# Batch 0's k loaded as fp32 by the SP queue and converted by VectorE, in a fused attention and feed-forward kernel on one core

## The chip, the cores and the metric

The kernel runs on one core of one Trainium2 chip. The metric is the device time of one execution in microseconds; lower is better. Before the change, three runs gave 164.0, 164.4 and 165.47 us, so the median is 164.4. One further execution was recorded by the hardware profiler; all rows shown here come from it.

## The reference

An attention over 32 learned memory slots, then a feed-forward layer with a maximum over three projections:

```python
batch, n_heads, seq, head_dim, n_mem = 8, 8, 576, 64, 32
a = softmax(phi, axis=slots)                       # fp32 [8, 8, 576, 32]
k_m = einsum('bhsm,bhsd->bhmd', a, k)
v_m = einsum('bhsm,bhsd->bhmd', a, v)
attn = softmax(q @ k_m.T / sqrt(head_dim), axis=slots)
x = (attn @ v_m)                                   # as [4608, 512]
h = max(x @ w1, x @ w2, x @ w3)                    # w1, w2, w3: [512, 768]
out = h @ w_out                                    # w_out: [768, 512]
```

All inputs and the output are fp32 in HBM. The matrix products run in bf16.

## The kernel before

**Tiling.** A batch has eight heads, taken as four pairs j. `by_pair` (L79) lays a batch of q, k, v or phi out as 128 partitions by four pairs; in each pair a partition holds nine rows in a row, for q, k and v 576 numbers, which is 2304 bytes of fp32. k and v go to `kvo`, a bf16 tile for each of two alternating batches; row 1 of it is k, row 0 is v, and row 2 is a column of ones. q goes to `qq`, phi to `ph` (fp32).

**Weights.** `w_sb` (L71) holds w1, w2 and w3 as bf16, as four pairs by three matrices by 768 columns, so that in each partition the three matrices alternate from pair to pair. `wo_sb` holds w_out. At the start of the run w3 is transposed on TensorE (step W, L186, matmuls at L192), and w3 times w_out is formed (step O, L197, matmuls at L200), which then serves all batches. w1 and w2 are needed by the folds (step D, matmuls at L445).

**Queues.** A load that converts fp32 to bf16 goes through the software DMA queue, which GpSimd (POOL) feeds; each such load is an instruction in GpSimd's own order. The SP queue carries phi of batch 0 (two halves, L92) and later every output row (L552). Both queues run on the same 16 DMA engines.

**Order.** The whole program is one hand-written list of steps (L621 on), each a letter, a number and a batch. The list fixes every engine's own order; an instruction then waits only for what it needs. The steps of the opening that matter here:

- E: the exponential of phi on ScalarE (L234).
- H0, H2 (`load_kv`, L96): the two halves of batch 0's k, pairs 0 and 1, then pairs 2 and 3. H1 and H3 are the halves of v. L3 (`load_q`, L108) loads q.
- Z: so many matmuls on a zero tile (`warm_up`, L163), which nothing reads.
- B0, N0, K0 (L243, L267, L297): the product of exp(phi) with k and the column of ones on TensorE (L254), its normalisation on VectorE, its transpose. B1, N1 and K1 do the same with v.
- Q0, Q1 (L311): transposes of q on VectorE (L318). S, M, R, X: scores, their exponential, sums and normalisation.
- Y2, Y3, Y0, Y1 (`load_w`, L115, and `load_wo`, L123): the loads of w3, w_out, w1, w2.
- G0 (`wait_for`, L128): a copy of two numbers of k on GpSimd, so that the loads issued behind it start only when batch 0's k has landed.
- L0 to L3: loads for the next batches.

GpSimd's order in the opening is therefore: k (two halves), q, the identity matrix and some constants, w3, the gate, w_out, v (two halves), w1, w2, then phi, k, q and v of batch 1.

Of the kernel before, what the change touches and what calls it, by code (L numbers as in the profile page):

```python
# [8 lines left out]
FP32 = mybir.dt.float32  # L9
# [6 lines left out]
def kernel(  # L16
# [12 lines left out]
    nc = tc.nc  # L29

    B, H, S, D = q.shape
# [5 lines left out]
    NC = S // HP  # L37
# [26 lines left out]
    kvos = []  # L64
# [6 lines left out]
    w_sb = const.tile([P, NP, 3, DF], BF16, name="w_sb")  # L71
# [5 lines left out]
    loaded = {}  # L77

    def by_pair(src, b):  # L79
        return src[b].rearrange("h s d -> (h s) d").rearrange(  # L80
            "(j p c) d -> p j (c d)", p=P, c=NC
        )

    halves = [slice(0, NP // 2), slice(NP // 2, NP)]

    def load_ph(b):
        ph = inp.tile([P, NP, NC, M], FP32, name="ph")
        loaded.setdefault(b, {})["ph"] = ph
        dst = ph.rearrange("p j c m -> p j (c m)")
        if b == 0:  # L90
            for h in halves:
                nc.sync.dma_start(out=dst[:, h], in_=by_pair(phi, b)[:, h])  # L92
        else:
            nc.gpsimd.dma_start(out=dst, in_=by_pair(phi, b))

    def load_kv(b, i, h=slice(0, NP)):  # L96
        kv = loaded.setdefault(b, {})["kv"] = kvos[b % 2]
        nc.gpsimd.dma_start(  # L98
            out=kv[:, 1 - i, h].rearrange("p j c d -> p j (c d)"),
            in_=by_pair((k, v)[i], b)[:, h],  # L100
        )

    def pack(b, i):
        nc.gpsimd.tensor_copy(  # L104
            out=kvrs[b % 2][:, :, :, D * i : D * (i + 1)], in_=kvos[b % 2][:, 1 - i]
        )

    def load_q(b):  # L108
        qq = inp.tile([P, NP, NC, D], BF16, name="qq")
        loaded.setdefault(b, {})["q"] = qq  # L110
        nc.gpsimd.dma_start(  # L111
            out=qq.rearrange("p j c d -> p j (c d)"), in_=by_pair(q, b)
        )

    def load_w(i):  # L115
        w = (moe_w1, moe_w2, moe_w3)[i]
        nc.gpsimd.dma_start(
            out=w_sb[:, :, i], in_=w.rearrange("(j p) f -> p j f", p=P)
        )
# [3 lines left out]
    def load_wo():  # L123
        nc.gpsimd.dma_start(out=wo_sb, in_=moe_w_out.rearrange("(t p) c -> p t c", p=P))
# [3 lines left out]
    def wait_for(b, n):  # L128

        x = loaded[b]["q"][0:1, 0, 0, 0:2] if n else loaded[b]["kv"][0:1, 1, NP - 1, 0, 0:2]  # L130
        nc.gpsimd.tensor_copy(out=gate, in_=x)
# [84 lines left out]
    def w_diff(n):  # L216

        lo, end = FIRST[n]
        nc.vector.tensor_tensor(
            out=w12[:, :, lo:end],  # L220
            in0=w12[:, :, lo:end],
            in1=w_sb[:, :, 2, lo % DF : lo % DF + end - lo],
            op=ALU.subtract,
        )
# [5 lines left out]
    def att_exp(b, js=slice(0, NP)):  # L230
        s = st.setdefault(b, {})
        if "e" not in s:
            s["e"] = work.tile([P, NP, NC, M], BF16, name="e")
        nc.scalar.activation(out=s["e"][:, js], in_=loaded[b]["ph"][:, js], func=AF.Exp)  # L234
# [8 lines left out]
    def att_kv(b, part=None):  # L243
        s = st[b]
        kvp = two_banks()
        s["kvp", part] = kvp
        kv = loaded[b]["kv"]
        nd = {None: 2 * D + 1, 0: 2 * D, 1: D}[part]
        kvr = kvrs[b % 2]
        for c in range(NC):  # L250
            for j in range(NP):
                for a in range(NG):
                    r = slice(HP * a, HP * (a + 1))
                    nc.tensor.matmul(  # L254
                        kvp[M * j : M * (j + 1), a, 0:nd],
                        lhsT=s["e"][r, j, c, :],
                        rhs={
                            None: lambda: kvr[r, j, c, 0:nd],
                            0: lambda: k_and_ones(kv, r, j, c),
                            1: lambda: kv[r, 0, j, c, :],  # L260
                        }[part](),
                        start=(c == 0),
                        stop=(c == NC - 1),
                        tile_position=(HP * a, M * j),
                    )
# [320 lines left out]
    def issue(b, n, swap):  # L586

        i = int(n[1:]) if len(n) > 1 else None
        {
            "I": lambda: [make_identity(nc, ident)]  # L590
            + [nc.gpsimd.memset(x[:, :, :, 2 * D : 2 * D + 1], 1.0) for x in kvrs],
            "Y": lambda: load_w(i) if i < 3 else load_wo(),
            "L": lambda: load_ph(b) if i == 0 else load_q(b) if i == 3 else load_kv(b, i - 1),
            "H": lambda: load_kv(b, i % 2, halves[i // 2]),
            "r": lambda: pack(b, i),
            "E": lambda: [att_exp(b, h) for h in (halves if b == 0 else [slice(0, NP)])],
            "B": lambda: att_kv(b, i),
            "N": lambda: att_kv_norm(b, i),
            "K": lambda: att_kv_t(b, swap, i),
            "Q": lambda: att_q(b, i),  # L600
            "S": lambda: att_score(b),
            "a": lambda: att_t(b, i),
            "s": lambda: att_sum(b, i),
            "c": lambda: att_rec(b, i),
            "m": lambda: att_mul(b, i),
            "X": lambda: (ones_mul if (b, i) in ONES else att_back)(b, i),
            "M": lambda: ones_sum(b, i),
            "R": lambda: ones_rec(b, i),
            "D": lambda: fold(b, i, swap),
            "F": lambda: ffn1(b, i, swap),  # L610
            "P": lambda: ffn2_head(b, i),
            "T": lambda: ffn2(b, i, swap),
            "W": lambda: w3_t(i, swap),
            "O": lambda: w3_o(i, swap),
            "V": lambda: w_diff(i),
            "G": lambda: wait_for(b, i),
            "Z": lambda: warm_up(i),
        }[n[0]]()


    for w in """  # L621
        E@0 H0@0 H2@0 L3@0 Z25@0 B0@0 I@0 N0@0 Z2@0 K0@0! Q0@0 Q1@0 Z9@0 S@0 Z2@0 M0@0 M1@0
        R0@0 Y2@0 G0@0 R1@0 W0@0 Y3@0 W1@0 W2@0 Z6@0 O1@0 H3@0 O3@0 O2@0 H1@0 X1@0 B1@0 X0@0
        N1@0 K1@0 O0@0 Y0@0 D1@0! D0@0! D3@0 F8@0 F10@0 F2@0 V0@0 F6@0 F0@0! Y1@0 D2@0 L0@1
        V2@0 L1@1 D4@0 V1@0 L3@1 F4@0 F3@0 L2@1 L1@2 F1@0 L2@2 F7@0 F5@0 F9@0 F11@0 P0@0 E@1
        B0@1 N0@1 T3@0 K0@1! Q0@1 Q1@1 L0@2 T0@0! S@1 L3@2 P1@0 V4@0 B1@1 a0@1 T1@0 s0@1 L3@3
        N1@1 c0@1 L2@3 a1@1 s1@1 K1@1 c1@1 m0@1 P2@0 X0@1 D1@1 D0@1 m1@1 D2@1 X1@1 T2@0! L1@3
        r0@2 F2@1! F10@1 F0@1! F4@1 F8@1 F5@1 r1@2 F6@1 L0@3 E@2 F9@1 F11@1 L0@4 L1@4 F1@1 F7@1
        P2@1 F3@1 B@2 N@2 D3@1 P3@1 P0@1 K@2! Q0@2 Q1@2 T0@1! S@2 a0@2 s0@2 c0@2 T4@1! m0@2
        a1@2 s1@2 c1@2 T2@1! D2@2 Q1@3 D0@2 D1@2! T3@1 m1@2 T1@1 X1@2 r1@3 L3@4 L2@4 X0@2 L2@5  # L630
        Q0@3 F4@2 F6@2 F0@2 F8@2 F7@2 r0@3 F1@2 F10@2 F5@2 E@3 F9@2 F11@2 F2@2 B@3 D3@2 N@3
        F3@2 L0@5 P3@2 K@3 P0@2 L1@5 S@3 T0@2 a0@3 r0@4 s0@3 c0@3 a1@3 s1@3 P2@2 m0@3 c1@3 D2@3
        m1@3 D1@3! L3@5 D0@3 T3@2! Q1@4 X0@3 X1@3 T2@2! Q0@4 T1@2 F10@3! r1@4 F2@3 F11@3 F6@3
        F8@3! F3@3 E@4 F4@3 F9@3 F5@3 F0@3 F7@3 B@4 D3@3 N@4 F1@3 P1@3 K@4 L1@6 L0@6 T1@3! r1@5
        E@5 S@4 D2@4 L2@6 a0@4 T4@3! r0@5 s0@4 L0@7 a1@4 P0@3 D1@4! B@5 s1@4 c1@4 D0@4 L1@7
        c0@4 Q1@5 m1@4 T0@3! N@5 Q0@5 K@5 P2@3 L2@7 X1@4 m0@4 S@5 X0@4 T2@3! F0@4 F2@4 a0@5
        F4@4! F6@4 r1@6 a1@5 P3@3 L3@6 D1@5! r0@6 D3@4 s1@5 D3@5! T3@3 F10@4 s0@5 c1@5 F3@4
        F8@4 c0@5 F11@4 F1@4 F7@4 F5@4 F9@4 m0@5 P1@4 P0@4 E@6 D0@5 m1@5 X0@5 B@6 D2@5 X1@5
        T0@4 T1@4 N@6 F6@5 F0@5 F7@5 F1@5 F4@5! Q0@6 F2@5 r0@7 F10@5 r1@7 T3@4! Q1@6 F5@5 F8@5!
        E@7 K@6! F9@5 T2@4! F3@5 S@6 F11@5 a1@6 B@7 L3@7 D2@6 N@7 a0@6 D0@6 T4@5! s0@6 K@7 Q1@7  # L640
        P0@5 s1@6 D1@7! D3@7 c1@6 c0@6 D0@7 Q0@7 m1@6 T0@5! m0@6 P1@5 S@7 T1@5 X1@6 a0@7 a1@7
        P3@5 X0@6 D2@7 D1@6! s0@7 c0@7 D3@6 s1@7 T3@5! m0@7 c1@7 F6@6 P2@5 m1@7 X0@7 X1@7 F10@6
        T2@5! F7@6 F10@7! F4@6 F0@7! F11@6 F8@6 F11@7 F0@6! F2@6 F5@6 F1@6 F3@6 F2@7! P3@6 F9@6
        P2@6 F1@7 F6@7 F7@7 T2@6 F4@7! T3@6! F8@7 T0@6! T1@6 F9@7 F5@7 F3@7 P0@7 T1@7! T0@7
        T2@7 T4@7! T3@7
    """.split():
        n, b = w.rstrip("!").split("@")
        issue(int(b), n, w.endswith("!"))
# [30 lines left out]
```

## Time and profile before

| | before |
|---|---|
| runs | 164.0, 164.4, 165.47 us |
| profiled execution, device time | 163.68 us |
| its span, first to last instruction | 161.9 us |
| TensorE matmul busy | 151.5 us, 94% of the span |
| VectorE / ScalarE / GpSimd busy | 106.4 / 88.5 / 69.6 us |
| DMA software queue | 16080 packets, 21.43 MB |
| DMA SP queue | 5728 packets, 9.90 MB |

The span is made of the instructions' own times; the device time has 1.8 us around it. A row of a timeline gives the start in us from the first instruction, the length, the engine, the line, the operation and its tiles; in brackets stands how long the engine was idle before and what ended that. The bytes of a software transfer are counted as written, that is as bf16. A window's row gives the busy time of each engine in a stretch, the clock that was granted to TensorE, the mean busy share of the 16 DMA engines (over 1 where packets overlap) and the rate in GB/s.

### The profile page before, as it was taken

The numbers are of one execution on the slowest core, as the hardware profiler recorded it, in microseconds if no ns is written. First come the engines' busy times: TensorE is split into PE (matmuls) and PEld (weight loads), VectorE is DVE, ScalarE is ACT, GpSimd is POOL, SyncE is SP. The second block draws the span as 40 slices with busy tenths as digits, with TensorE's granted clock in tenths as the row PEclk, the third lists the DMA queues.
The fourth block names the chain that finished last, engine by engine and source line by source line (L and its number), as shares of the span: only waits on it lengthen the run. The fifth ranks groups of instructions, "written<-read, shape, count | busy, mean of one in ns | idle before, by whom it ended". The sixth has DMA issues, their size and how long they took to land.

```text
span 161.9 us, 4816 instructions
## 1 busy us (share of the span) xinstructions
PE 151.5 (94%) x2056; PEld 85.6 (53%) x2080; DVE 106.4 (66%) x203; ACT 88.5 (55%) x129; POOL 69.6 (43%) x72
## 2 busy tenths in 40 slices
PE   7988799999899999999999999999999999999990
PEld 2443344664376436744774465656653467655450
DVE  2041704898969583959896959856897779863520
ACT  3206246926484769748567878477278963112010
POOL 7295213101879069746975914995004240000000
PEclk9999999999999999999999999999999999999999
DMA  5999999999999999999999999995911330024133
GB/s 152 176 203 201 203 211 214 276 208 208 260 312 236 208 244 382 282 212 215 314 278 208 292 287 306 235 208 140 188 72 65 130 112 21 0 84 158 74 143 132
DMA packets 21974, 31.77 MB, mean 196 GB/s; under 512 B 1216, under 2 KB 16576, under 8 KB 21952
## 3 DMA queue, kind: packets, MB, share of 16 engines
q0 software_dynamic: 16080, 21.43, 69.2%
q1 hardware_dynamic: 5728, 9.90, 17.4%
q8 instruction: 16, 0.26, 0.7%
q10 hardware_dynamic: 144, 0.13, 0.2%
q14 instruction: 6, 0.05, 0.1%
HBM read 39.32 MB, written 9.44 MB: 301 GB/s over the span
## 4 chain that ended last, share of the span: by engine, by line
PE 80%; DMA 10%; ACT 2%; issue 2%; DVE 2%; POOL 1%; ACTq 0%; POOLq 0%
PE psum L471 28%; PE psum L532 19%; PE psum L541 8%; PE psum L502 8%; DMA wo_sb<-in_moe_w_out_dram 7%; PE psum L445 6%; DMA kvo<-in_k_dram 4%; PE psum L254 4%; PE psum L200 3%; PE psum L338 2%; PE psum L522 1%; DVE sm L400 1%; PE psum L563 1%; ACT h L178 1%; PE psum L303 1%
## 5 line engine op out<-in xcount | busy, mean ns | idle before, releaser
L471 PE MATMUL psum<-attn,wp 128*128 128x288 bf16 x384 | 51.1, 286 | 0.1
L471 PEld LDWEIGHTS <-wp 128*128 128x128 bf16 x384 | 37.0, 98 | 14.1 <-issue 1.1
L484 DVE TENSOR_TENSOR hT<-psum,h 128x576 bf16<-128x576 f32 x48 | 34.2, 751 | 10.8 <-PE psum L471 9.8
L532 PE MATMUL psum<-wo_sb,hT 128*128 128x512 bf16 x131 | 34.1, 380 | 1.5 <-issue 1.4
L180 ACT CAST wp<-psum 128x1024 bf16<-128x1024 f32 (+1 forms) x30 | 28.2, 991 | 9.0 <-PE psum L445 7.2
L104 POOL COPY kvr<-kvo 128x2304 bf16<-128x2304 bf16 x12 | 25.3, 2112 | 10.5 <-PE psum L541 5.8
L178 ACT ACTIVATE h<-psum 128x576 bf16<-128x576 f32 x35 | 21.7, 661 | 14.3 <-PE psum L471 14.1
L180 ACT COPY ot<-psum 128x512 f32<-128x512 f32 x24 | 14.2, 596 | 22.8 <-PE psum L541 13.6
L414 POOL TENSOR_TENSOR t<-t,sm 128x576 bf16<-128x576 bf16 x14 | 16.1, 1155 | 22.7 <-DVE sm L409 22.4
L532 PEld LDWEIGHTS <-hT 128*128 128x128 bf16 x144 | 12.6, 98 | 16.7 <-issue 5.3
L541 PE MATMUL psum<-wp,attn 128*128 128x512 bf16 x62 | 18.4, 379 | 0.1
L502 PE MATMUL psum<-wo_sb,hT 128*128 128x512 bf16 x58 | 16.8, 379 | 0.5 <-issue 0.2
L167 PE MATMUL psum<-warm 128*128 128x512 bf16 x42 | 12.2, 447 | 1.4 <-DVE warm L136 1.2
L347 ACT ACTIVATE e<-psum 128x576 bf16<-128x576 f32 x16 | 9.6, 657 | 5.7 <-PE psum L338 5.7
L318 DVE STREAM_TRANSPOSE qT<-qq 128x576 f32<-128x576 f32 x16 | 11.8, 750 | 0.8 <-DMA qq<-in_q_dram 0.8
L182 DVE TENSOR_SCALAR h<-psum 128x576 bf16<-128x576 f32 x13 | 9.8, 752 | 3.2 <-PE psum L471 1.9
L111 POOL DMA_DIRECT2D qq<-in_q_dram x8 | 6.2, 774 | 12.8 <-DVE qT L318 7.6
L184 DVE COPY ot<-psum 128x512 f32<-128x512 f32 x11 | 7.5, 681 | 6.4 <-PE psum L541 4.4
L234 ACT ACTIVATE e<-ph 128x1152 bf16<-128x1152 f32 (+1 forms) x9 | 9.5, 1056 | 2.2 <-DMA ph<-in_phi_dram 2.2
L400 DVE TENSOR_REDUCE sm<-t 128x18 f32<-128x576 bf16 x14 | 10.4, 742 | 0.3
L541 PEld LDWEIGHTS <-attn 128*128 128x128 bf16 x62 | 6.1, 98 | 7.2
L98 POOL DMA_DIRECT2D kvo<-in_v_dram x9 | 6.7, 744 | 7.0 <-PE psum L254 4.0
(61 smaller groups left out, 135.5 us busy)
## 6 DMA issues: line engine op xcount, KB each, us to landing
out_dram<-ot SPq DMA_DIRECT2D x35, 256.0 KB, 5.4
qq<-in_q_dram POOLq DMA_DIRECT2D x8, 576.0 KB, 12.2
ph<-in_phi_dram POOLq DMA_DIRECT2D x7, 576.0 KB, 15.3
kvo<-in_k_dram POOLq DMA_DIRECT2D x7, 576.0 KB, 18.5
kvo<-in_v_dram POOLq DMA_DIRECT2D x7, 576.0 KB, 16.9
w_sb<-in_moe_w_dram POOLq DMA_DIRECT2D x3, 768.0 KB, 15.1
wo_sb<-in_moe_w_out_dram POOLq DMA_DIRECT2D x1, 768.0 KB, 10.7
ph<-in_phi_dram SPq DMA_DIRECT2D x2, 288.0 KB, 3.1
```

What stands on the lines that cost most here:

```text
L104: nc.gpsimd.tensor_copy(out=kvrs[b % 2][:, :, :, D * i : D * (i + 1)], in_=kvos[b % 2][:, 1 - i])
L167: nc.tensor.matmul(po[:, 0:BANK], lhsT=warm[:, 0:P], rhs=warm, start=True, stop=True)
L178: nc.scalar.activation(out=out_, in_=in_, func=AF.Relu)
L180: nc.scalar.copy(out=out_, in_=in_)
L318: nc.vector.transpose(out=s["qT"][:, j].rearrange("p j c r e -> p (j c r e)").bitcast(FP32), in_=loaded[b]["q"][:, j].rearrange("p j c d - ...
L400: nc.vector.tensor_reduce(out=sm, in_=s["t", g].rearrange("p n r e -> p n e r"), op=ALU.add, axis=mybir.AxisListType.X,)
L414: nc.gpsimd.tensor_tensor(out=t, in0=t, in1=s["sm", g].unsqueeze(2).to_broadcast([P, S // HP, R, 2]), op=ALU.mult,)
L471: nc.tensor.matmul(acc[:, h, 0:SH], lhsT=wps[b][:, g, w * DF + ft * P : w * DF + (ft + 1) * P], rhs=attn[:, g, c0 : c0 + SH], start=(g == ...
L484: nc.vector.tensor_tensor(out=hT[:, ft, (b % 2) * S : (b % 2 + 1) * S].rearrange("p (h n) -> p h n", h=2), in0=a, in1=s["h1", ft], op=ALU.max,
L502: nc.tensor.matmul(po, lhsT=hT[:, fc, c0 : c0 + P], rhs=wo_sb[:, fc, :], start=(n == 0), stop=False,)
L532: nc.tensor.matmul(po, lhsT=hT[:, fc, c0 : c0 + P], rhs=wo_sb[:, fc, :], start=(n == 0 and t < 4), stop=(n == FT - 1 and t == 4),)
L541: nc.tensor.matmul(po, lhsT=attn[:, g, c0 : c0 + P], rhs=wp3s[b][:, g, :], start=False, stop=(g == NG - 1),)
```

## The change

Batch 0's k no longer goes through the software queue. Two transfers on the SP queue, behind the two of phi, bring its halves as fp32 into the part of `w_sb` that is later filled with w1 and w2; four VectorE copies, one for each pair, convert it into `kvo`. GpSimd's first load is now q. The first warm-up has 23 matmuls rather than 25. In the order of VectorE the copies stand ahead of the first normalisation, N0.

```diff
+    k32 = w_sb[:, :, 0:2].rearrange("p j i f -> p j (i f)").bitcast(FP32)
+    k32 = k32[:, :, 0 : NC * D]
+
+    def load_k32(h):
+
+        nc.sync.dma_start(
+            out=k32[:, h], in_=by_pair(k, 0)[:, h]
+        )
+
+    def cast_k32(j):
+        kv = loaded.setdefault(0, {})["kv"] = kvos[0]
+        nc.vector.tensor_copy(out=kv[:, 1, j], in_=k32[:, j].rearrange("p (c d) -> p c d", c=NC))
...
+            "A": lambda: load_k32(halves[i]),
+            "C": lambda: cast_k32(i),
...
-        E@0 H0@0 H2@0 L3@0 Z25@0 B0@0 I@0 N0@0 Z2@0 K0@0! Q0@0 Q1@0 Z9@0 S@0 Z2@0 M0@0 M1@0
+        E@0 A0@0 A1@0 L3@0 Z23@0 C0@0 C1@0 C2@0 C3@0 B0@0 I@0 N0@0 Z2@0 K0@0! Q0@0 Q1@0 Z9@0 S@0 Z2@0 M0@0 M1@0
```

The rest of the list is the same. In each pair of `w_sb` the staged k takes the first 1152 of the 1536 bf16 columns of w1 and w2; w3's columns of a pair follow behind these. In the changed program the load of w3 (Y2) waits for both transfers of k and for the fourth copy.

## The prediction

> **What bounds the kernel now.** I first read the engines' shares: TensorE is busy for 94% of the span, so nearly all of the run is TensorE work in a row, and only a stage in which TensorE waits can move the end. The chain of waits, cut to its first microseconds (start, length, what), says where that stage is:
>
> ```profile
> 1.25 0.88 POOL kvo L98
> 2.13 6.18 DMA kvo<-in_k_dram
> 8.37 0.12 POOL gate L131
> 8.49 10.72 DMA wo_sb<-in_moe_w_out_dram
> 19.21 0.14 issue
> 19.35 4.04 PE psum L200 x18
> ```
>
> Up to 19.35 us the end is set by transfers: k, the gate, then w_out, which TensorE's step O (L200) waits for. Behind it TensorE runs on with hardly a gap to 161.9. The timeline of TensorE, and GpSimd's lines from the same stretch, say who waits for which load (start, length, engine, line, operation, and in brackets the idle time before and its releaser):
>
> ```profile
> 1.19 7.92 PE L167 MATMUL psum<-warm 128*128 128x512 bf16 x25 [1.19 <-DVE warm L136]
> 9.04 0.80 PE L254 MATMUL psum<-kvo,e 64*32 64x128 bf16 x72
> 14.21 0.95 PE L359 MATMUL psum<-e,blkones 128*128 128x288 bf16 x4 [0.27 <-ACT e L347]
> 15.49 1.51 PE L192 MATMUL psum<-ident,w_sb 128*128 128x128 bf16 x24 [0.34 <-DMA w_sb<-in_moe_w_dram]
> ...
> 4.27 0.76 POOL L117 DMA_DIRECT2D w_sb<-in_moe_w_dram  x1
> 8.37 0.17 POOL L131 COPY gate<-kvo 1x2 bf16<-1x2 bf16 x1 [3.34 <-DMA kvo<-in_k_dram]
> 8.49 0.82 POOL L124 DMA_DIRECT2D wo_sb<-in_moe_w_out_dram  x1
> ```
>
> w3 (L117) is issued at 4.27 and waits for nothing; TensorE takes it at 15.49. GpSimd issues w_out at 8.49, long before the transfers ahead of it are through, so the gate's wait costs nothing: the software queue is full. The windows show that (window, its length, busy time and count of five engines, granted clock, DMA share, GB/s):
>
> ```profile
> 2.00:4.00 2.00, 2.00 (x6) 0.76 (x5) 0.00 (x0) 0.24 (x2) 1.93 (x5) 1.00 0.97 290
> 4.00:8.00 4.00, 4.00 (x15) 1.64 (x14) 0.00 (x0) 1.14 (x2) 1.02 (x4) 1.00 1.15 176
> 10.00:15.00 5.00, 4.21 (x50) 1.60 (x49) 2.11 (x5) 1.87 (x4) 3.73 (x6) 1.00 1.17 204
> ```
>
> From 2 us on the DMA engines have no hole: phi by SP's queue (to about 4.1), then k, q, w3, w_out, v, w1 and w2 one behind the other, some 176 to 204 GB/s as written. So the opening is a stream of transfers; a change there is worth what it adds to that stream ahead of w_out.
>
> **The change part by part.** *k itself.* Two software transfers of 288 KB (as bf16) become two hardware ones of 576 KB (fp32). The bytes read are the same. Both queues use the same 16 engines; a stretch where an output leaves by SP while a load comes in shows how they share (packets of each queue, 2.5 us, 41.75 to 44.25):
>
> ```profile
> q0 software_dynamic: 234, 0.26, 60.6%
> q1 hardware_dynamic: 236, 0.45, 53.5%
> ```
>
> They alternate packet by packet. k is 512 rows of 2304 bytes, q 512 rows as well, so the two finish together: 512/235 x 2.5 = 5.4 us, plus about 0.35 because an output packet has 2048 bytes and one of k's 2304: 5.8 us. They begin at about 4.1: SP's k is issued directly behind phi (0.44 us each, so by 2.6), and the first software packets of before, too, came only as phi ended. So k is complete at about 9.9 and, since the engines do not all end together, landed at 10.3 (9.8 to 10.9), against 8.31 before. The 2.0 us are q's share, which used to come behind k.
>
> *The casts.* Four VectorE copies, 128x576 fp32 to bf16, run in SBUF; the first two lie under the second half's transfer, two stand behind it. The trace has no such copy. Above: the transposes of the same 128x576 fp32 (L318), 0.72 to 0.75 us each; below: L219, two-input bf16 at 0.64 us for 1024 elements, 0.36 for 576. One operand is like the first and one like the second, so I take the middle, 0.55: 1.1 us for two (0.7 to 1.5). VectorE is idle from 1.9 to 9.9, so nothing else is displaced. End of casts 11.4.
>
> *The first k matmuls (L254)* move from 9.04 to about 11.5, and with them the normalisation and scores; before, the scores' last sums (L359, 14.21 + 0.95) ended 6.1 us behind the start of L254, so they would now end at 17.6. q is no bound: it lands by 10.9, and its transposes come 1.7 us behind L254.
>
> *The w3 load, the main term.* The fp32 k is kept in the space of w1 and w2 in w_sb, whose rows interleave with w3's. In the instruction list of the changed program the w3 load on GpSimd waits for both k transfers and for the fourth cast; before it waited for nothing. Behind it in GpSimd's queue stand the gate, w_out, both halves of v, w1, w2 and all loads of batch 1. So w3 is issued at 11.4 rather than 4.27, and q has drained by then: the software queue is empty and has to start anew. That has a price in two places of this trace, transfers of 576 KB issued into an empty software queue. The first is k, 1.25 to 8.31: 7.1 us. The second is the last q: its row in GpSimd's timeline, its issue to landing, and the windows in which it comes in:
>
> ```profile
> 110.75 0.80 POOL L111 DMA_DIRECT2D qq<-in_q_dram  x1
> DMA to landing us min/median/max: 6.9/6.9/6.9
> 112.00:113.00 1.00, 1.00 (x7) 0.47 (x5) 0.49 (x1) 1.00 (x2) 0.00 (x0) 1.00 0.73 57
> 113.00:114.00 1.00, 1.00 (x10) 0.71 (x9) 0.67 (x2) 0.36 (x1) 0.00 (x0) 1.00 1.01 142
> 114.00:115.00 1.00, 0.95 (x11) 0.76 (x10) 1.00 (x3) 0.48 (x1) 0.00 (x0) 1.00 1.16 199
> ```
>
> The DMA share in the windows falls to 0.08 at 111.5 to 112.0, the transfer comes in only after 112, and three windows pass before the usual 199 GB/s. w3 is 768 KB, 197 KB (at 200 GB/s 1.0 us) more than those: 7.0 + 1.0 = 8.0 us, taken as 7.9 from the 6.9 case, which is the one with a queue that had already been in use. Landed at 11.4 + 7.9 = 19.3, against 4.27 + 11.2 (its issue to landing) = 15.5 before: +3.8.
>
> The Trainium skill (DMA: Bandwidth & Descriptors, Anatomy of one DMA — SWDGE (gpsimd) path) gives a transfer of this kind about 2.0 us plus its bytes over 436 GB/s. For w3's 1.57 MB as read that is an estimate of 5.6 us, by which the sum would be +1.5. By that rule q's 1.18 MB would have taken 4.7 us; the trace has 6.9 and disagrees.
>
> *What follows w3.* w_out is issued 0.8 us behind w3 and runs directly behind it, as before (19.2 - 15.5 = 3.7 us): landed at 23.0 rather than 19.2. TensorE is ready sooner: the w3 transposes start with w3 at 19.4 and need 2.6 us with their evictions (15.49 to 18.04), to 22.0. So step O starts +3.8 late. v, w1 and w2 follow in the same order, each +3.8, and so does the place where w2 is again awaited (29.86). Nothing later can make it up, as TensorE has no gaps there; batch 1's loads are late by as much as TensorE is.
>
> *Small edits.* Two warm-up matmuls fewer (25 to 23, 0.22 us each) end the warm-up at 8.6; that is idle time now. GpSimd saves one issue (0.8 us) that it then waits out. SP's output transfers use other semaphores, whose earlier users are done. Nil.
>
> Sum: +3.8 us. The profiled execution took 163.68 (span 161.9, 1.8 around it), so it would be 167.5; the median of the runs shown, 164.4, lies 0.7 above it, and gives 168.2. I predict 167.9.
>
> **The rivals.** *A, not slower: SP's queue is served first.* If q's packets come late or yield to k, k is through at phi's rate: 1.18 MB at about 345 GB/s (334, 373 and 330 GB/s from 2.5 to 4.0) is 3.4 us, landed at 7.5; casts to 8.6. q then runs from 7.5 to 10.6, and w3, issued at 8.6, has its first packet 1.5 to 1.75 us later (as at 110.75), while q still runs. No hole, w3 where it was: 163.7 to 164.4. It decides if the casts end before about 8.9. For it: before, no software packet came while phi was running. Against it: the even 234 to 236. 8%.
>
> *B, the queue restarts more cheaply.* If w3 begins 1.5 to 1.75 us behind its issue and at full rate from then (no ramp as in 112 to 114), it starts at 13.0. Before, it began between the ends of q on the first and the last engine: q landed at 2.85 + 8.4 = 11.25, and k's landing at 8.31 was 1.2 behind what its rate gives (4.1 + 3.0), so between 10.1 and 11.25, about 10.6. That is +2.4, with the low ends of k and casts +1.4. Time 165.1 to 166.8, middle 166.1. For it: k's start at 4.0 showed no ramp, though it came 2.75 us behind its issue. Against it: both landings, 6.9 and 7.1 us. The rule for one transfer that is cited above from the Trainium skill (DMA: Bandwidth & Descriptors) is of this kind. 13%.
>
> *C, TensorE falls back to its slow pace.* The warm-up ran at 0.43 us a matmul up to 5.4 us and at 0.22 behind that. TensorE would now idle from 8.6 to 11.5. If it is slow again after that, the nine fillers ahead of the scores cost 9 x 0.21 = 1.9 us, the scores end at 20 instead of 17.6, and w3's transposes begin at 20 instead of 19.4; slow transposes may add 1.5 more, and O could start up to 1.5 us behind w_out: 168 to 169.7. The Trainium skill (TensorE: Matmul & The Clock Gate, What's actually happening) puts the return to half clock after an idle window of about 3.4 us. By that rule 2.9 us do not reach it; k's late end, 10.9, would. 5%.
>
> **How the numbers follow.** The forecast itself has 74%. Its ends: k at 9.8, casts 0.7, 7.9: +2.9; k at 10.9, casts 1.5: +4.8. With the two bases (163.68 and 164.4) that is 166.6 to 169.2. The range reaches down into B, to 165.3, and up to 169.3; it leaves out A, some of B and C, and runs beyond the ends. A run of this kernel tells 1% (1.6 us) from no change. Slower by over 1% (beyond 166.0): the forecast, C and half of B, 0.84. Within: most of A and the rest of B, 0.14. Faster by over 1%: the part of A in which q's earlier arrival would speed up something that I have as covered, 0.02.
>
> **What would show it.** w3's load issued at 11 to 12 us and the DMA share near zero for over a microsecond before it; k landed after 10 with as many packets of q as of k before that; cast rows of 0.36 to 0.75 us; L254 near 11.5; L192 near 19.4 and L200 near 23.2, behind DMA; from there the same work in the same time. It is wrong if k lands before 8, if w3's transfer starts without a hole, or if L200 starts before 21.

## The result, and the profile after

Six runs of the changed kernel took 170.66 us (169.49 to 173.09), six of the kernel before 164.76 (164.0 to 165.47). The ratio is 1.035, with a 95% interval of 1.030 to 1.039: slower. One of the six, 173.09, was a slow execution, over 1.5% above the fastest, and is left out of the ratio. The forecast was 167.9, with a range of 165.3 to 169.3, so the direction was right and the time lies above the range. The profiled execution took 170.91 us with a span of 169.1, against 163.68 and 161.9 before. In the rows of after, every line number behind the new functions is 13 higher: the k matmuls are L267 (L254 before), the w3 transposes L205 (L192), step O L213 (L200), w3's load L130 (L117).

The chain of waits of after, from its eighth step on (start, length, what), has the shape that the prediction gave it, but starts with a k that lands almost three microseconds later than forecast:

```profile
2.23 10.95 DMA w_sb<-in_k_dram
13.19 0.02 issue
13.21 0.84 DVE kvo L114 x2
14.05 0.30 issue
14.35 0.76 POOL w_sb L130
15.11 0.12 POOL gate L144
15.24 10.68 DMA wo_sb<-in_moe_w_out_dram
25.91 0.14 issue
26.05 4.04 PE psum L213 x18
```

Step by step against the forecast: k landed at 13.2 (forecast 10.3), the two casts that stand behind it took 0.84 (1.1), and GpSimd needed another 0.3 to get going (0 in the forecast). From w3's issue to w_out's landing it took 25.91 - 14.35 = 11.6 us, the forecast's 7.9 + 3.7, though its two parts came out otherwise, as is said below. So O starts at 26.05, where the forecast had 23.2 and the kernel before 19.35. Of the 7.2 us by which the span grew, 6.7 are there when O starts.

The timelines of TensorE and VectorE in after show who waits (idle time before and its releaser in brackets):

```profile
11.86 0.66 PE L267 MATMUL psum<-kvo,e 64*32 64x128 bf16 x4 [3.99 <-DVE kvo L114]
13.72 1.51 PE L267 MATMUL psum<-kvo,e 64*32 64x128 bf16 x68 [1.21 <-DVE kvo L114]
...
16.33 2.93 PE L180 MATMUL psum<-warm 128*128 128x512 bf16 x9
...
21.35 1.51 PE L205 MATMUL psum<-ident,w_sb 128*128 128x128 bf16 x24
...
26.05 4.04 PE L213 MATMUL psum<-wo_sb,w3T 128*128 128x512 bf16 x18 [1.89 <-DMA wo_sb<-in_moe_w_out_dram]
```

```profile
11.34 0.83 DVE L114 CAST kvo<-w_sb 128x576 bf16<-128x576 f32 x2 [9.45 <-DMA w_sb<-in_k_dram]
13.21 0.83 DVE L114 CAST kvo<-w_sb 128x576 bf16<-128x576 f32 x2 [1.04 <-DMA w_sb<-in_k_dram]
...
22.01 1.89 DVE L197 COPY w3T<-psum 128x1024 bf16<-128x1024 bf16 x3 [4.58 <-PE psum L205]
```

Two things are to be seen. The casts are short and only wait for k. And there is a second chain, hardly earlier than the first: from the late k through the k matmuls, the fillers (warm-up matmuls that nothing reads) and the scores TensorE comes to the w3 transposes at 21.35, with no gap over 0.34 us behind 13.72, and their evictions end at 22.01 + 1.89 = 23.9. w3 itself landed at 21.30; TensorE's load of it waited 0.2 us, so the two chains meet there. Had w_out been there at any time, O could not have started before 23.9. In this execution the wait for w_out is therefore the last 2.2 us at most of O's delay of 6.7; the rest, to within the 0.2, TensorE's own late work, at the clock that it had, would have brought as well.

Where k lost the time is read from the windows (granted clock, DMA share and GB/s are the last three columns):

```profile
4.00:5.00 1.00, 1.00 (x5) 0.45 (x4) 0.00 (x0) 0.29 (x1) 0.00 (x0) 1.00 0.77 167
...
9.00:10.00 1.00, 0.00 (x0) 0.00 (x0) 0.00 (x0) 0.00 (x0) 0.00 (x0) 1.00 1.11 315
10.00:11.00 1.00, 0.00 (x0) 0.00 (x0) 0.00 (x0) 0.00 (x0) 0.00 (x0) 1.00 0.56 161
11.00:12.00 1.00, 0.14 (x2) 0.10 (x2) 0.66 (x2) 0.00 (x0) 0.00 (x0) 0.58 0.20 58
12.00:13.00 1.00, 0.43 (x4) 0.10 (x2) 0.17 (x1) 0.00 (x0) 0.00 (x0) 0.50 0.10 36
...
14.00:15.00 1.00, 0.92 (x67) 0.87 (x65) 0.04 (x1) 0.00 (x0) 0.65 (x1) 0.50 0.00 0
...
16.00:17.00 1.00, 1.00 (x5) 0.50 (x5) 1.00 (x3) 0.37 (x1) 1.00 (x3) 0.50 0.84 68
17.00:18.00 1.00, 1.00 (x3) 0.30 (x2) 0.43 (x1) 0.00 (x0) 1.00 (x2) 0.51 1.06 178
```

The hole is there, from 13 to 16 us and partly from 10. What was not expected is the stretch from 10.5 to 13.2: a share of 0.20 and then 0.10 is as much as three and then one or two of the sixteen engines at work. The trace also records when a transfer lands, in sixteen events that no view prints, read here as one for each engine. For the second half of k the first comes at 10.31 and the fourteenth at 11.92; the last two come at 12.99 and 13.19, and only then has k landed. The packets of each queue in two stretches, 4 to 8 us (first fence) and the last two microseconds, 11 to 13.2 (second fence), complete it:

```profile
q0 software_dynamic: 306, 0.35, 57.1%
q1 hardware_dynamic: 256, 0.55, 43.7%
```

```profile
q0 software_dynamic: 17, 0.01, 4.0%
q1 hardware_dynamic: 39, 0.08, 9.6%
```

The queues did share the engines about packet for packet, as forecast. But in these 4 us 562 packets came in, 141 per microsecond, where the forecast had counted on 1024/5.8 = 177. The count rises from 113 in the first microsecond to 166 in the fourth and reaches 172 and 176 in the next two. That leaves the two queues (177 - 141) x 4 = 144 packets, 0.8 us, behind the forecast. And 56 packets, some 5% of the two transfers, come between 11.0 and 13.2.

### The profile page after: what moved, and what is told of

It reads as the page before. It is cut to its first block, busy times and chain, and to the rows that moved or that the text cites. A ratio compares the mean times of both kernels' runs of the same rounds, so it can differ in the third digit from the quotient of the medians.

```text
span 169.1 us, 4819 instructions
## 1 busy us (share of the span) xinstructions
PE 152.8 (90%) x2054; PEld 86.1 (51%) x2078; DVE 107.7 (64%) x207; ACT 88.5 (52%) x129; POOL 68.4 (40%) x70
## 4 chain that ended last, share of the span: by engine, by line
PE 78%; DMA 13%; DVE 2%; issue 2%; ACT 1%; SPq 1%; POOL 1%; ACTq 0%
PE psum L484 28%; PE psum L545 18%; PE psum L554 8%; PE psum L515 7%; DMA w_sb<-in_k_dram 6%; DMA wo_sb<-in_moe_w_out_dram 6%; PE psum L458 5%; PE psum L267 3%; PE psum L213 3%; PE psum L351 2%; PE psum L535 1%; DVE sm L413 1%; PE psum L576 1%; PE psum L316 1%; SPq L92 1%
## 5 line engine op out<-in xcount | busy, mean ns | idle before, releaser
L117 POOL COPY kvr<-kvo 128x2304 bf16<-128x2304 bf16 x12 | 25.3, 2113 | 9.3 <-DMA kvo<-in_v_dram 6.8
L267 PEld LDWEIGHTS <-e 64*32 64x32 bf16 x720 | 7.5, 93 | 9.0 <-issue 7.7
## 6 DMA issues: line engine op xcount, KB each, us to landing
w_sb<-in_moe_w_dram POOLq DMA_DIRECT2D x3, 768.0 KB, 15.1
w_sb<-in_k_dram SPq DMA_DIRECT2D x2, 576.0 KB, 10.3
```

The costliest lines, as they stand in the source:

```text
L117: nc.gpsimd.tensor_copy(out=kvrs[b % 2][:, :, :, D * i : D * (i + 1)], in_=kvos[b % 2][:, 1 - i])
L267: nc.tensor.matmul(kvp[M * j : M * (j + 1), a, 0:nd], lhsT=s["e"][r, j, c, :], rhs={None: lambda: kvr[r, j, c, 0:nd], 0: lambda: k_and_one ...
```

## The experiments

At the start there were two theories of the loss. W: w3's wait for the staging space is the whole loss, the prediction's main term. K: k's own late landing costs as much through the second chain. The first four kernels separate these and the way k and q share the engines. All ratios are to the kernel before, run on the same chip in the same session (medians 164.11, 164.14 and 163.94 us).

**1. The same, but staged where nothing waits for it.** The fp32 k goes into the `kvo` tile of the other batch, so w3 waits for nothing.

```diff
-    k32 = w_sb[:, :, 0:2].rearrange("p j i f -> p j (i f)").bitcast(FP32)
-    k32 = k32[:, :, 0 : NC * D]
+    k32 = kvos[1][:, 0:2].rearrange("p i j c d -> p (i j c d)").bitcast(FP32)
+    k32 = k32.rearrange("p (j x) -> p j x", j=NP)
```

> The fp32 k is staged in batch 1's k and v tile, which is empty until later, so the w3 load waits for nothing again; everything else as in the changed kernel. Theory W (the added wait of w3 is the whole loss): 164 to 165.5 us, w_out landed near 19. Theory K (k's own late landing, 13.2 us, is a second chain that ends only 2 us before the first): k still lands at 12 to 14, step O starts at 23 to 24.5 instead of 26.0, and the time is 168 to 169.5 us.

Measured: 169.66 us (169.32 to 171.75), ratio 1.037 (1.030 to 1.043): above both theories' times. The changed kernel has 1.035 (1.030 to 1.039), so nothing was gained that these runs can tell. w3 was issued at 2.83 us, so its wait was gone. The chain of waits of this run's profile, cut at 30 us:

```profile
2.23 13.78 DMA kvo<-in_k_dram
16.01 0.02 issue
16.04 0.84 DVE kvo L114 x2
16.88 0.04 issue
16.92 1.14 PE psum L267 x66
...
26.14 1.24 PE psum L180 x5
27.38 2.81 PE psum L213 x13
```

No weight load stands in it any more; it goes from k through TensorE's own work to O. k now shares the engines with q and with w3 and landed at 16.0, 2.8 us later than in the changed kernel and outside K's 12 to 14; so this run doesn't show what the wait alone is worth (kernels 6 and 7 do). Theory W as the whole cause falls.

**2. k alone, q behind it.** In the changed kernel the gate and q's load are put behind the fourth cast, so nothing shares the engines with k.

```diff
-        E@0 A0@0 A1@0 L3@0 Z23@0 C0@0 C1@0 C2@0 C3@0 B0@0 I@0 N0@0 ...
+        E@0 A0@0 A1@0 I@0 Z23@0 C0@0 C1@0 C2@0 C3@0 G0@0 L3@0 B0@0 N0@0 ...
```

> As the changed kernel, but q's load is issued only behind the fourth cast, so k has the DMA engines to itself after phi. Theory C (k is late because its packets alternate with q's): k lands at 7.4 to 8.2 us. Theory S (a transfer of 2304-byte fp32 rows is slow by itself, or some engines are): k lands at 10 or later. With C: q lands near 15.6, w3 near 19.3, w_out near 23.0, time 168 to 169 us; with S: q, w3 and w_out later by the same as k, time above 171.

Measured: 170.23 us (169.88 to 172.5), ratio 1.037 (1.035 to 1.040); the profile is of the longest execution, 172.5, and only its first 11 us are read here. The casts' rows and two windows:

```profile
8.61 0.83 DVE L114 CAST kvo<-w_sb 128x576 bf16<-128x576 f32 x2 [6.72 <-DMA w_sb<-in_k_dram]
10.04 0.83 DVE L114 CAST kvo<-w_sb 128x576 bf16<-128x576 f32 x2 [0.60 <-DMA w_sb<-in_k_dram]
```

```profile
8.00:9.00 1.00, 0.00 (x0) 0.00 (x0) 0.39 (x2) 0.00 (x0) 0.00 (x0) 1.00 0.11 44
9.00:10.00 1.00, 0.46 (x4) 0.18 (x4) 0.44 (x2) 0.00 (x0) 0.00 (x0) 1.00 0.04 16
```

k landed at 10.0, so sharing costs it 3.2 us. But by 8.3 us nearly all of it was in: of the sixteen landing events of the second half fourteen came by 8.31, the last two at 9.07 and 10.02, with no other transfer beside them. The late engines are no effect of q alone. So C's 7.4 to 8.2 was missed and S's landing, "at 10 or later" because some engines are slow, was met; S's time, above 171, was not.

**3. The late issue by itself, in the kernel before.** There the gate is put ahead of w3, so w3 waits for the bf16 k and all else is as it was.

```diff
-        R0@0 Y2@0 G0@0 R1@0 W0@0 Y3@0 ...
+        R0@0 G0@0 Y2@0 R1@0 W0@0 Y3@0 ...
```

> The kernel before, with only the w3 load moved behind the gate, so that it waits for k (software, landed 8.3 us) as in the changed kernel. Theory D (a wait costs only if the software queue drains; q still runs to 11.2): w3 is issued at 8.5, lands at 15 to 15.6 as before, time 164.2 to 165.3 us. Rival (a late issue costs the queue's start, 2.6 us, in any case): w3 lands at 17 or later, time 166.5 to 167.5 us.

Measured: 165.59 us (165.47 to 165.72), ratio 1.009 (1.008 to 1.011), a little above theory D's range and below the rival's. w3 was issued at 8.99 and q was still coming in, yet the rate fell to 150 GB/s in the window of 10 to 11 and to 111 in the next, against 209 and 206 before. O started at 20.56, +1.2. So a w3 issued at about 9 costs 1.5 us even while q runs. In this profile k and q also landed 0.5 us later than before (8.81 and 11.80), which can be part of O's delay.

**4. Staged elsewhere, q behind the first half of k.** To kernel 1 a wait of GpSimd for two numbers of k's first half is added, ahead of q's load.

```diff
+        if n == 2:
+            nc.gpsimd.tensor_copy(out=gate, in_=k32[0:1, 0, 0:2])
+            return
...
-        E@0 A0@0 A1@0 L3@0 Z23@0 ...
+        E@0 A0@0 A1@0 I@0 G2@0 L3@0 Z23@0 ...
```

> The fp32 k staged elsewhere as in the run above, and q's load held until the first half of k has landed; w3 right behind q. Theory C (sharing with q makes k late): k lands at 7.4 to 8.8 us, L254 runs near 9, q is issued near 6 and lands near 13, w3 near 16.8, w_out near 20.6: 165.5 to 166.7 us. Theory S: k lands at 10 or later, time above 167.

Measured: 168.06 us (167.56 to 168.41), ratio 1.024 (1.022 to 1.027): theory C missed, and S's two figures met. The first half of k landed only at 8.7 us, so q was issued at 9.20 in place of near 6, and landed at 15.1; k landed at 10.14, O started at 23.89.

The next three ask whether the queue or the fp32 form is to blame, and how k and q can share without the late landing.

**5. The fp32 k and the casts, but by the software queue**, ahead of q as before, staged as in kernel 1.

```diff
-        nc.sync.dma_start(
+        nc.gpsimd.dma_start(
             out=k32[:, h], in_=by_pair(k, 0)[:, h]
         )
```

> k is still fp32, staged elsewhere and converted by VectorE, but loaded by the software queue ahead of q, so no second queue runs beside it. Theory Q (the second queue is what makes k late): k lands at 8 to 9.5 us, casts 0.84 us behind it, w3 lands at 15 to 16 with no wait, time 164.3 to 166 us. Rival F (fp32 rows of 2304 bytes are slow on some engines whatever the queue): k lands at 10 or later, time above 166.5.

Measured: 165.04 us over ten runs (164.41 to 165.87), ratio 1.005 (1.001 to 1.008). k landed at 9.78, w3 was issued at 4.31, O started at 20.36. So Q's time was met, and k's landing lies a little above its 8 to 9.5: one engine's event came at 9.78, the other fifteen by 8.59. The fp32 form, its staging and the four casts cost 0.5%, 0.8 us, together; what is left of the change's loss is in k's place on a second queue beside q and in the wait of w3.

**6. Staged elsewhere, q behind phi.** As kernel 4, with the wait on phi instead of k's half.

```diff
+        if n == 2:
+            nc.gpsimd.tensor_copy(out=gate, in_=loaded[b]["ph"][0:1, NP - 1, 0, 0:2])
+            return
```

> As the run with k staged elsewhere (w3 waits for nothing), but q's load is issued when phi has landed, near 4.5 us, so its packets come in near 7, when k by the SP queue is half through. Theory Q: k lands at 9.5 to 11 us, between the 10.0 of k alone and the 13 to 16 of full sharing; q near 12, w3 near 16, w_out near 20; time 164.8 to 166.8 us. Rival (sharing does not matter, the lateness varies from run to run): k lands at 12 or later, time above 167.5.

Measured: 166.12 us (165.99 to 166.47), ratio 1.012 (1.008 to 1.016). q was issued at 4.53, k landed at 9.88, O started at 21.52: k's landing and the time are theory Q's. O waited here for the last engine: w_out's fifteenth landing event came at 20.02, the last at 21.39.

**7. The changed kernel with q behind phi.** The wait of kernel 6, but k staged in `w_sb` again, so w3 waits for it. This puts k's landing near the one that the prediction had assumed, and leaves everything else of the prediction in force.

> The changed kernel with its staging in w_sb and so with w3's wait, but with q's load issued only when phi has landed. k lands near 10 to 11 as the prediction had assumed. Theory P (the prediction's chain is right and only k's landing was mis-sized): w3 issued at 11 to 12, landed 7 to 8 us later, w_out near 23, time 167 to 168.8 us. Rival (the wait of w3 costs nothing of its own): the time equals that of the run with k staged elsewhere and q behind phi, to within 0.5 us.

Measured: 167.56 us (167.25 to 167.86), ratio 1.020 (1.016 to 1.024). Its chain, and step O in its timeline:

```profile
2.23 7.33 DMA w_sb<-in_k_dram
9.56 0.02 issue
9.58 0.84 DVE kvo L114 x2
10.43 0.30 issue
10.72 6.96 DMA w_sb<-in_moe_w_dram
```

```profile
22.25 4.04 PE L216 MATMUL psum<-wo_sb,w3T 128*128 128x512 bf16 x18 [1.40 <-DMA wo_sb<-in_moe_w_out_dram]
```

k landed a little before the 10 to 11 that was expected. From there the prediction's chain holds: the wait, the hole (88 and 34 GB/s in the windows from 11 to 13), w3 7.0 us behind its issue, w_out 4.4 behind that. With the 0.84 and 0.3 of above and the forecast's 7.9 and 3.7, a k at 9.56 puts O at 22.3; it started at 22.25. Against kernel 6, which differs by the staging alone, w3's wait costs 167.56 - 166.12 = 1.4 us; 0.7 of it are there when O starts in the two profiles.

**8. Kernel 1 without the idle TensorE.** Sixty fillers instead of 23 keep TensorE busy until k is there (`Z23@0` becomes `Z60@0`).

> The run with k staged elsewhere and q at once, with 60 rather than 23 warm-up matmuls, so that TensorE is busy until the second half of k has landed (16.0 us there). Theory H (the half clock after the idle time is on the path there, because step O waits for TensorE and not for w_out): granted clock 1.0 throughout, the fillers ahead of the scores take 2.1 instead of 3.4 us, time 1.5 to 2.2 us less than that run's 169.66. Rival (the clock is hidden behind transfers): within 0.5 us of it.

Measured: 170.53 us (169.27 to 170.81), ratio 1.037 (1.031 to 1.042), the same ratio as kernel 1's. The clock was at full rate throughout the opening, and the nine fillers of the scores took 2.10 us instead of 3.43, but the gain of theory H did not come. k landed at 14.5 here and at 16.0 in kernel 1; each is one profile, so this pair can't say what the clock was worth.

**9. The changed kernel without the idle TensorE** (`Z23@0` becomes `Z47@0`). Rival theory H: the half clock that the windows show from 11 to 18 us is part of the loss.

> The changed kernel with 47 rather than 23 warm-up matmuls, so that TensorE stays busy until k has landed (13.2 us). Theory T (step O waits for w_out, which hangs on k's landing and w3; the half clock from 11 to 18 us lies beside that wait): the fillers ahead of the scores take 2.1 instead of 2.9 us, w_out lands as before near 25 to 26, time within 1 us of the changed kernel's 170.66. Rival H (the half clock is part of the loss): 168.5 to 169.5 us.

Measured: 172.55 us (171.63 to 172.87), ratio 1.048 (1.042 to 1.054), slower than the changed kernel's 1.035, not faster, so theory T's time, within 1 us of 170.66, was missed too. In its timeline the w3 transposes now wait for w3, and O for w_out:

```profile
21.29 1.51 PE L205 MATMUL psum<-ident,w_sb 128*128 128x128 bf16 x24 [1.11 <-DMA w_sb<-in_moe_w_dram]
25.73 4.04 PE L213 MATMUL psum<-wo_sb,w3T 128*128 128x512 bf16 x18 [1.64 <-DMA wo_sb<-in_moe_w_out_dram]
```

k landed at 13.2 as before and O started at 25.73, 0.3 earlier than at half clock: TensorE's slow pace lay beside the wait for the weights, and H falls. The time by which this kernel is slower (172.87 against 170.91 in the two profiled executions) comes behind O. In its profile TensorE waited 1.24 us for w1: fifteen of its landing events came by 32.16, the last at 33.52, where the changed kernel had 32.15 and 32.52. Why all four runs are slower with more fillers stays open.

**10. Half rows.** The late engines could come from the long rows: SP's packets have 2304 bytes, and an engine that is behind has long ones left (L). Or the two queues take turns by packets whatever their size, and what is late stays late (R). k's four transfers now have 1152 bytes a row.

```diff
-        nc.sync.dma_start(
-            out=k32[:, h], in_=by_pair(k, 0)[:, h]
-        )
+        for x in (slice(0, NC * D // 2), slice(NC * D // 2, NC * D)):
+            nc.sync.dma_start(out=k32[:, h, x], in_=by_pair(k, 0)[:, h, x])
```

> The changed kernel with each half of k in two transfers of half rows, so that k's packets have 1152 bytes, as many as q's have when written, and there are 1024 of them to q's 512. Theory R (the queues take turns by packets, and an engine that falls behind stays behind): q is through earlier, when k is about half done, k's landing stays at 12 to 14.5 us, time 169.5 to 172 us. Rival L (the long rows make the engines fall apart): k lands at 11.5 or earlier, time below 169 us.

Measured: 171.64 us (171.25 to 171.79), ratio 1.044 (1.040 to 1.049). In 4 to 8 us 354 packets of the software queue came with 287 of SP's, and k landed at 13.28, in the changed kernel 13.2. L falls: with half the bytes in each of k's packets q came in 1.4 us earlier (issue to landing 10.0 us against 11.4), and k no earlier.

## Why the prediction was right or wrong

**The step that failed** is the landing of k: "k is complete at about 9.9 and, since the engines do not all end together, landed at 10.3 (9.8 to 10.9)". It was 13.2, and 13.2 to 13.3 in each of the three profiles in which k shares with a q issued at the start and with nothing else (after, kernels 9 and 10). Two terms of it were too small. The rate of 177 packets per microsecond was taken from a stretch in which both queues were already running; behind phi it was reached only after four microseconds, which puts the two queues 0.8 us behind. The rest, about 2 us, is the spread of the engines beyond the 0.4 that the forecast had for it: the middle of the sixteen landing events lies at 10.9, the last at 13.19. Kernel 2 shows such a spread with no q there: fourteen events by 8.3, the last at 10.0. The prediction itself had a row of this kind, k's landing of before, 1.2 us behind its rate, and used it only for rival B. That k's landing, and not a later step, makes the difference to the forecast is shown by kernel 7: with k at 9.56 the changed kernel takes 167.56. That this is so near the 167.9 of the forecast is in part luck, as the forecast had k at 10.3. What puts an engine behind is not shown: neither the packets nor the landing events carry an engine's name. It begins early, though: of the first half of k fourteen events came by 9.17 and two at 10.43 and 11.32, in kernel 2 fourteen by 6.86 and two at 7.62 and 8.59.

**The sharing of the engines** was right: 306 to 256 packets in the first four microseconds and 152 to 196 in the next two, from 8 to 10; in kernel 10, with packets of half the size, 287 to 354.

**The casts** were right in place and a little high: 0.84 for two (0.7 to 1.5 forecast), the low end.

**w3's wait and the restart** were right in mechanism: the hole from 13 to 16 us, and w3 and w_out together 11.6 us behind the issue, as forecast. That the sum agrees is luck. w3 landed 6.95 us behind its issue in place of 7.9, and 6.96 in kernel 7, so the 1.0 us that the forecast added for its size was not there; w_out then took longer, 4.6 for 3.7. The forecast left out 0.3 us that GpSimd needed from the last cast to the issue.

The estimate of 5.6 us from the Trainium skill (DMA: Bandwidth & Descriptors, Anatomy of one DMA — SWDGE (gpsimd) path) is not met by these 6.95; the measurement decides.

**What follows w3** was right for the chain but told half: "TensorE is ready sooner" no longer held by a margin of several microseconds, as k's delay moved TensorE's own work too (evictions of w3 at 23.9, O at 26.05). This is why kernel 1, which takes the wait away, gains nothing that the runs can tell, where the forecast's main term was 3.8 us; k, which then shares with w3 too, was later still. With k at 9.6 to 9.9 the price of the wait is 1.4 (kernels 6 and 7).

**The sum.** By the forecast's own chain, k is 2.9 later than forecast, the casts 0.3 shorter, GpSimd's 0.3 is new and the sum of the two weights is as forecast: O at 23.2 + 2.9 = 26.1, measured 26.05, 6.7 behind its start before. On 163.68 that is 170.4; 170.91 was measured. The last 0.5 come behind O and were not followed further. Between the medians the loss is 5.9.

**The rivals.** A (SP served first) is out: q's packets came as often as k's, and k landed at 13.2. B (a cheap restart) is out in the changed kernel: two windows without traffic and then three at 24, 68 and 178 GB/s. C came true as a mechanism: the warm-up ended at 7.9 rather than 8.6, TensorE stood idle for 3.99 us rather than 2.9 and was granted 0.50 of its clock afterwards, and the nine fillers took 2.93 us instead of 2.10; but at full clock, in kernel 9, O started only 0.3 us earlier.

The Trainium skill (TensorE: Matmul & The Clock Gate, What's actually happening) puts the fall to half clock behind an idle window of about 3.4 us; the 3.99 us here, with a granted clock of 0.58 in the window from 11 to 12, agree with it. Kernels 5, 6 and 7 had half clock with no idle time over 1.0 us (last section); for those the measurement decides.

**The signs that were named** held for the issue of w3 behind an empty stretch, for the packets and for the casts. The k matmuls, forecast near 11.5, came at 11.86 for the first four matmuls and at 13.72 for the rest, w3's transposes at 21.35 instead of 19.4, and O at 26.05 instead of 23.2: each by k's delay.

No kernel tried beat the one before; the nearest, kernel 5, is 0.5% above it.

## What to carry to other kernels

The load of k was there when the last of its sixteen landing events came, 1.3 us behind the fourteenth and 2.3 behind the middle: read the spread between the last packets and the mean rate from a transfer of the same kind, and give it a term of its own, above all where two queues share the engines. When a wait is on the path, work out also when the consumer would have been ready without it; here that was 2 us earlier, and a chain of its own from the same late load, so taking the wait away in kernel 1, where k landed later still, gained nothing that could be measured. Storage that is borrowed from a later load joins that load's issue to the last reader, and the queue that ran empty here took microseconds until it delivered again (24, 68 and 178 GB/s from 15 to 18 us).

## What the hardware showed that had not been expected

*Late engines.* Alone on the SP queue k landed about 2 us behind the bulk of its bytes (kernel 2); with the software queue beside it from the start at 13.2, with w3 there as well at 14.5 and 16.0 (kernels 8 and 1). Issued 3.3 us later, behind phi, the same q cost k nothing: 9.56 and 9.88 (kernels 7 and 6) against 10.0 alone, each from one profile. In kernel 6 it looks as if one engine stayed late: for w3, w_out, both halves of v, w1 and w2 the last landing event came 1.3 to 1.4 us behind the fifteenth each time.

*Half clock without a long idle time.* In kernel 7 TensorE was never idle for more than 0.9 us between 4 and 17 us, and yet the clock fell to half for three microseconds. The windows (TensorE's busy time is the second number, its clock the third from the end):

```profile
8.00:9.00 1.00, 0.68 (x5) 0.18 (x3) 0.83 (x2) 0.00 (x0) 0.00 (x0) 1.00 1.10 260
9.00:10.00 1.00, 0.23 (x2) 0.09 (x2) 0.42 (x2) 0.00 (x0) 0.00 (x0) 1.00 1.19 204
10.00:11.00 1.00, 0.76 (x68) 0.62 (x67) 0.41 (x2) 0.00 (x0) 0.28 (x1) 1.00 0.95 161
11.00:12.00 1.00, 0.75 (x28) 0.19 (x11) 0.70 (x3) 0.00 (x0) 1.00 (x3) 1.00 0.50 88
12.00:13.00 1.00, 0.86 (x4) 0.38 (x5) 0.64 (x2) 0.37 (x1) 1.00 (x2) 0.68 0.81 34
13.00:14.00 1.00, 1.00 (x4) 0.43 (x3) 0.89 (x2) 0.00 (x0) 1.00 (x3) 0.50 0.90 147
```

Four microseconds at 0.6 of the busy time, with short gaps and small matmuls (64 rows by 32 columns), came ahead of it. The nine fillers took 3.79 us there instead of 2.10. Kernels 5 and 6 show the same: TensorE busy 0.33 of the time from 8 to 11 us in kernel 5 and 0.58 from 8 to 12 in kernel 6, no gap over 1.0 us, and a clock of 0.50 in the window from 13 to 14. So in these three runs a stretch of little work was followed by half clock as one long gap was; whether the small share of busy time or the small matmuls did it is not shown.
